# One transformer block on one core: the order of the attention steps chosen by the next piece of side work, and paired maxima in every unit from the third on

## The chip, the cores and the metric

The kernel runs on 1 core of one Trainium2 chip. The metric is the device time of one execution in microseconds (us), given as the median over several executions. A core has five engines that run side by side and meet only at semaphores: TensorE (PE in the profile, its weight loads PEld), VectorE (DVE), ScalarE (ACT), GpSimd (POOL) and SyncE (SP, which here issues DMAs). Matrix products land in PSUM, which has eight banks of 128 partitions by 512 fp32 numbers; DVE and ACT read them from there, POOL and the DMAs can't.

## The reference

A block with adaptive layer norm: attention over 2048 rows of width 576 with 32 heads of 18 columns, then a gated feed-forward layer with 4608 hidden columns.

```
mod = (silu(c) @ w_mod) -> sa, ca, ga, sb, cb, gb
h = layernorm(x) * (1 + ca) + sa
q, k, v = split(h @ wqkv)             # 32 heads of 18
p = softmax(q @ k.T * 18 ** -0.5)     # 2048 x 2048 for each head
x = x + ga * ((p @ v) @ wo)
h = layernorm(x) * (1 + cb) + sb
x = x + gb * ((sigmoid(h @ w_gate) * (h @ w_up)) @ w_down)
```

The softmax needs the maximum of each row of scores before the exponentials can be taken. The kernel works in fp32 accuracy; where it uses the faster fp32r products, an operand is split into a high and a low part.

## The kernel before

**Units and steps.** Attention goes in 32 units. A unit is two heads and one half (1024) of the query rows; units 0 to 15 hold the first half of the rows, 16 to 31 the second. A unit has 16 steps (`kt`), one for each 128 keys. A step makes four score tiles of 128 keys by 512 queries (two heads, two query chunks, L1016) and takes their exponentials on ACT (L1020); the products with the values (L585) follow two steps behind (`LAG`). Units pass in the loop `for u in range(UNITS)`, steps in `for kt in range(NT)`. Each odd step closes a pair of steps, and the order of the work in the even and in the odd step is written out as a string of letters:

- `t`: one score tile and its exponential. `m`: one turn of the maxima (below).
- `v`: the products with the values for a whole step; `a`, `b`: the same for the first and the second 256 queries of each chunk.
- `w`, `s`: a place where side work is put in. `c`: the rest of that side work. `k`: the copy of the finished accumulator `o` out of PSUM on ACT (L602, `taken`), which is due once in a unit.

TensorE and ScalarE run in the order of the program here (`manual_schedule`); the order on VectorE and GpSimd is chosen by the framework's scheduler.

**Three orders.** `PLAIN` units use `("vtmmttmvtm", "tmttkwmctmm")`, `HALVED` units `("vmmtmmtsactt", "wmcmbkttmtmt")`, and units 30 and 31 a third one with `TURNED`. The tuples at the head of the file fix which unit is which: halved are 1 to 15 and 21 to 27.

**Maxima.** The generator `maxima` (L455 on) runs ahead of attention by one unit and 24 turns: a turn is one score tile of 128 queries by 512 keys, computed the other way round (L480), and its maximum on DVE (L486). Four turns belong to a step, so eight to a pair. In a unit outside `SINGLE`, two of the eight chunks are paired: the first is a product with differences of keys, ACT takes its positive part into `over` (L489), and one DVE instruction adds this to the second chunk and takes the maximum (L491). So a paired group of eight costs DVE seven instructions and ACT one more; an unpaired one costs DVE eight. `SINGLE` holds units 0, 1, 17 to 20 and 29. At the end of a unit `spread` (L507 on) transposes the maxima and sends them by DMA into the rows of the query tile.

**Banks.** Score tiles, maxima tiles and all side work take turns in seven PSUM banks (`bank`), in order of issue: a new tile has to wait until the tile seven before it has been read. The eighth bank is the accumulator `o`.

**Side work.** `outputs` (four transposes, L612) brings a finished unit's result into rows at step 3 of the next unit. From step 240 (`FROM0`, unit 15) on, one piece of `first_rows` is taken in each pair of steps: eleven pieces that load and split the output weights on POOL (`load_wo`); for each of the 8 row tiles of the first half four pieces of `project_o` (transposes of the row tile, L699, and their copy by DVE, L705; one more transpose, L716; two groups of 14 products, L732, each ended by a DVE addition, L734); eight pieces of statistics; the scales of the layer norm, whose power runs on POOL (L196); and twelve sets of four transposes (L842) with pieces on POOL between them. From step 457 (`FROM1`, unit 28) on, the pieces of `last_rows_project` follow: three for each of the 8 row tiles of the second half (three transposes, then two groups of 9 products). In a pair all of this stands in the odd step, at `w`.

Of the kernel before, what the change touches and what calls it, by code (L numbers as in the profile page):

```python
# [37 lines left out]
HW = S // 2  # L38
UNITS = H
LEAD = 6  # L40
FROM0, FROM1 = 15 * 16, 28 * 16 + 9
DL = 384
ORDER = (1, 6, 2, 7, 5, 4, 3)
LOOK = 4
# [2 lines left out]
LAG = 2  # L47

MAXIMA = ((1, 0), (0, 0), (1, 1), (0, 2), (1, 2), (0, 3), (0, 1), (1, 3))
PLAIN = (0, 16, 17, 18, 19, 20, 28, 29)  # L50
SINGLE = (0, 1, 17, 18, 19, 20, 29)
HALVED = tuple(range(1, 16)) + tuple(range(21, 28))
MAXIMA_H = ((1, 0), (0, 0), (1, 1), (0, 2), (0, 3), (1, 2), (0, 1), (1, 3))
SIDES_H = ((1, 0), (1, 1), (0, 1), (0, 0))
SIDES = ((0, 0), (0, 1), (1, 0), (1, 1))
TURNED = ((0, 1), (0, 0), (1, 1), (1, 0)), ((0, 1), (1, 1), (0, 0), (1, 0))
ORDERED = 7
SEVENS = NB - 2
TURNS = {1: 1, 6: 2, 2: 4, 7: 3, 5: 5, 4: 7, 3: 6}
# [5 lines left out]
def tile_block(ctx, tc, x_in, wqkv, wo, w_gate, w_up, w_down, c_in, w_mod, out):  # L65
# [389 lines left out]
    def maxima():  # L455


        n = HW // P
        last = None
        for u in range(UNITS):  # L460
            qs, ks = heads(u)
            mx = mxs[u % 2]
            if u not in SINGLE and u - 2 in SINGLE:
                nc.gpsimd.memset(mx[:, 0:n, 1], LOWEST)
            for i in range(8 * n):
                if last is not None and i == (9 if u == 1 else 8):
                    if u == 1:
                        for _ in spread(*last):
                            pass
                    else:  # L470
                        state["spread"] = last
                qt = i // 8
                beside = (64 * u + i - 64 - 4 * LEAD) // 64
                pairs = u not in SINGLE or u in (17, 29) and beside in HALVED
                h, kc = (MAXIMA_H if beside in HALVED else MAXIMA)[i % 8]
                rows = slice(64 * h, 64 * h + 3 * DH)
                paired = pairs and h == 0 and kc < 2
                at = NCH if paired and kc == 0 else kc
                sp = bank()
                nc.tensor.matmul(  # L480
                    sp, qs[rows, qt * P : (qt + 1) * P],
                    ks[rows, at * 512 : (at + 1) * 512], start=True, stop=True,
                )
                to = mx[:, h * n + qt, kc : kc + 1]
                if not paired:
                    nc.vector.tensor_reduce(to, sp, axis=AX.X, op=ALU.max)  # L486
                elif kc == 0:
                    over = small.tile([P, 512], F32, name="over", bufs=1)
                    nc.scalar.activation(over, sp, AF.Relu)  # L489
                else:  # L490
                    nc.vector.tensor_tensor_reduce(  # L491
                        out=over, in0=sp, in1=over, scale=1.0, scalar=LOWEST,
                        op0=ALU.add, op1=ALU.max, accum_out=mx[:, h * n + qt, 0:1],
                    )
                if i < 8 * n - 1:
                    yield
            nm = small.tile([P, 2, n], F32, name="nm")
            nc.vector.tensor_reduce(
                nm.rearrange("p h t -> p (h t)"), mx, axis=AX.X, op=ALU.max, negate=True
            )  # L500
            last = (qs, nm)
            yield
        for _ in range(8):
            yield
        state["spread"] = last
# [175 lines left out]
    def project_o(t):  # L681

        wo_h, wo_l, we = weights
        if t <= 8:
            held_rows[:] = temp([P, 2048], F32R), temp([P, 2048], F32)
        T, T_ = held_rows
        if t < 8:
            xt, full, od = T_[:, 0:D], T_[:, 1024:1536], T_[:, 1536:1664]
        else:
            T, T_ = T[:, 1024 * (t % 2) : 1024 * (t % 2) + 1024], T_[:, 960 * (t % 2) : 960 * (t % 2) + 960]  # L690
            xt, full = T_[:, 0:D], T_[:, D : D + 384]
        nc.gpsimd.dma_start(xt, x_rows[:, t, :])
        src = Os[t // 8][:, t % 8, :]
        n = 4 if t < 8 else DL // P
        oh = T[:, 0 : n * P]
        ol = T[:, 512 : 512 + n * P]
        pt = bank()
        for i in range(n):
            nc.tensor.transpose(pt[:, i * P : (i + 1) * P], src[:, i * P : (i + 1) * P], ident)  # L699
        if t >= 12:  # L700
            nc.vector.tensor_copy(oh, pt[:, 0 : n * P])
            nc.vector.tensor_sub(ol, pt[:, 0 : n * P], oh.bitcast(F32))
        else:
            full = full[:, 0 : n * P]
            nc.vector.tensor_copy(full, pt[:, 0 : n * P])  # L705
            nc.gpsimd.tensor_copy(oh, full)
            nc.gpsimd.tensor_sub(ol, full, oh.bitcast(F32))
        yield
        if t < 8:
            om = T[:, 1024:1152]  # L710
            omh = T[:, 1152:1280]
            nc.gpsimd.tensor_copy(
                od.rearrange("p (a e) -> p a e", e=64), src[:, DM:D].unsqueeze(1).to_broadcast([P, 2, 64])
            )
            pt = bank()
            nc.tensor.transpose(pt[:, 0:P], od, ident)  # L716
            nc.vector.tensor_copy(od, pt[:, 0:P])
            nc.gpsimd.tensor_copy(om[0:64], od[0:64])
            nc.gpsimd.tensor_copy(omh[64:P], od[64:P])
            nc.gpsimd.tensor_sub(om[64:P], od[64:P], omh[64:P].bitcast(F32))  # L720
            yield
        for h in range(2):
            cols = slice(h * HALF, (h + 1) * HALF)
            ts_ = []
            for i in range(n):
                a, b = oh[:, i * P : (i + 1) * P], ol[:, i * P : (i + 1) * P]
                ts_ += [(a, wo_h[:, i, cols]), (a, wo_l[:, i, cols]), (b, wo_h[:, i, cols])]
            if t < 8:
                ts_ += [(om, we[:, 0, cols]), (om, we[:, 1, cols])]
            acc = bank()  # L730
            for i, (a, w) in enumerate(ts_):
                nc.tensor.matmul(acc[:, :HALF], a, w, start=i == 0, stop=i == len(ts_) - 1)  # L732
            to = Oa[:, t, :] if t < 8 else xt
            nc.vector.tensor_add(to[:, cols], xt[:, cols], acc[:, 0:HALF])  # L734
            yield
        if t >= 8:
            nc.gpsimd.dma_start(x1p[:, t - 8, :], xt)

# [227 lines left out]
    for u in range(UNITS):  # L966
# [6 lines left out]
        for kt in range(NT):  # L973
            step = u * NT + kt
            turns["to"] = 64 + 4 * LEAD + 4 * (step + 1)
            kcols = slice(kt * P, (kt + 1) * P)
            plain = u in PLAIN
            halved = u in HALVED
            sides = iter(SIDES if plain else SIDES_H if halved else TURNED[kt % 2])
            probs = [None] * 4  # L980
            order = ("vtmmttmvtm", "tmttkwmctmm") if plain else ("vmmttmmtvt", "mtkttmwmcmt")
            if halved:
                order = ("vmmtmmtsactt", "wmcmbkttmtmt")
            for does in order[kt % 2]:
                if does == "m":
                    turn()
                elif does == "k":
                    taken()
                elif does == "w":
                    if kt == 3:  # L990
                        follow.append(outputs())
                        next(follow[-1], None)
                    if "spread" in state and not halved:
                        follow.append(spread(*state.pop("spread")))
                        next(follow[-1])
                    if FROM0 <= step < FROM1:
                        next(rows0, None)
                    if step >= FROM1:
                        next(rows1, None)
                elif does == "s":  # L1000
                    if "spread" in state:
                        follow.append(spread(*state.pop("spread")))
                        next(follow[-1])
                elif does == "c":
                    while follow:
                        next(follow.pop(0), None)
                elif does == "v":
                    if step >= LAG:
                        values()
                elif does in "ab":  # L1010
                    values(slice(0, 256) if does == "a" else slice(256, 512))
                else:
                    c, h = next(sides)
                    sT = bank()
                    rows = slice(64 * h, 64 * h + 3 * DH + 2)
                    nc.tensor.matmul(  # L1016
                        sT, ks[rows, kcols], qs[rows, c * 512 : (c + 1) * 512], start=True, stop=True
                    )
                    pr = probs[2 * c + h] = ppool.tile([P, 512], F32, name=f"p{2 * c + h}")
                    state["exp"] = nc.scalar.activation(pr, sT, AF.Exp, scale=SCALE)  # L1020
# [678 lines left out]
```

## Time and profile before

| | us |
|---|---|
| median of 3 executions | 2830.45 |
| lowest, highest | 2825.56, 2831.19 |
| the profiled execution | 2833.97 |
| its span, first to last instruction | 2832.2 |

The profiled execution stands 3.5 us above the median. Its span has three parts: normalising and the projections to q, k and v up to about 237 us, attention up to about 1555 us, and the feed-forward layer after that. The page gives for each engine the time in which it was busy and its share of the span; the groups of instructions give busy time, mean duration of one in ns, and the idle time in front of them with what ended it. The chain is the sequence of work that ended last, followed back from the end. A windows row gives, for one stretch of the span, its length, the busy time of each engine with the number of instructions, the granted TensorE clock and the share of the DMA engines. Matrix products overlap in the pipeline, so their single durations are longer than the spacing at which they follow each other.

### The profile page before, as it was taken

The page shows a single profiled execution, that of the slowest core. Times are in us where ns is not written, and L with a number is a line of the kernel's source. Part 1 is how long each engine was busy: PE and PEld are TensorE (multiplying, and loading weights), DVE is VectorE, ACT ScalarE, POOL GpSimd, SP SyncE. Part 2 cuts the span into 40 slices and gives each one's busy share as a digit, 9 for nine tenths or more (in the row PEclk, how much of TensorE's full clock was granted, in tenths as well). Part 3 has the DMA queues.
Part 4 walks back from the last instruction along what each step waited for, and adds up shares of the span by engine and source line. Part 5 has one row for each costly group of instructions (what it writes and reads, how often), then busy time and mean ns, then how long its engine had stood idle before and what let it go on. Part 6 is the DMA issues. An engine that isn't in the chain of part 4 may idle for free.

```text
span 2832.2 us, 50132 instructions
## 1 busy us (share of the span) xinstructions
PE 2788.0 (98%) x18293; PEld 1843.5 (65%) x18293; DVE 2315.3 (82%) x4367; ACT 1592.1 (56%) x3020; POOL 821.5 (29%) x1088
## 2 busy tenths in 40 slices
PE   7999999999999999999999999999999999999999
PEld 5974444444444444444443888888888888888888
DVE  7278999999998988999982878888898677777777
ACT  3216999999997678999888322333333222222221
POOL 3125208787842111662013222222221100000000
PEclk9999999999999999999999999999999999999999
DMA  5344225544432120221125866667767966666663
GB/s 171 126 150 148 69 58 171 171 171 164 181 108 78 36 58 23 105 100 58 36 75 176 295 212 226 236 216 272 275 249 275 351 200 195 199 198 196 199 198 111
DMA packets 170119, 462.55 MB, mean 163 GB/s; under 512 B 21196, under 2 KB 87760, under 8 KB 159760
## 3 DMA queue, kind: packets, MB, share of 16 engines
q1 hardware_dynamic: 148768, 358.36, 37.8%
q0 software_dynamic: 21104, 100.98, 10.0%
q8 instruction: 144, 2.36, 0.3%
q14 instruction: 103, 0.84, 0.1%
HBM read 281.92 MB, written 176.82 MB: 162 GB/s over the span
## 4 chain that ended last, share of the span: by engine, by line
PE 92%; DVE 4%; DMA 2%; ACT 1%; issue 1%; POOL 0%; SPq 0%; DVEq 0%; POOLq 0%; ACTq 0%
PE x L1145 26%; PE o L585 19%; PE s L1016 12%; PE s L480 11%; PE d L1295 8%; PE d L1227 6%; PE s L301 4%; PE s L732 2%; PE s L352 2%; DMA out_dram<-Oa 1%; PE s L612 1%; DVE mx L486 1%; ACT p L1020 1%; DVE Oa L1299 0%; DMA wm<-in_w_mod_dram 0%
## 5 line engine op out<-in xcount | busy, mean ns | idle before, releaser
L1020 ACT ACTIVATE p<-s 128x512 f32<-128x512 f32 x2048 | 1075.0, 620 | 134.5 <-PE s L1016 74.3
L486 DVE TENSOR_REDUCE mx<-s 128x1 f32<-128x512 f32 x1636 | 1033.2, 684 | 103.3 <-PE s L480 88.6
L585 PE MATMUL o<-p,vaug 128*32 128x256 f32 (+1 forms) x5504 | 587.6, 497 | 5.0 <-ACT oT L602 4.6
L480 PE MATMUL s<-k,q 54*128 54x512 f32 x1920 | 533.7, 434 | 1.9 <-DVE mx L486 1.6
L1016 PE MATMUL s<-q,k 56*128 56x512 f32 x1920 | 533.1, 446 | 0.2
L1016 PEld LDWEIGHTS s<-q,k 56*128 56x128 f32 x1920 | 257.9, 185 | 275.8 <-DVE mx L486 99.7
L480 PEld LDWEIGHTS s<-k,q 54*128 54x128 f32 x1920 | 281.6, 185 | 213.2 <-DVE mx L491 146.7
L1145 PE MATMUL x<-k,w 128*128 128x512 f32 x1512 | 369.7, 392 | 2.4 <-ACT w L1126 2.4
L1145 PEld LDWEIGHTS x<-k,w 128*128 128x128 f32 x1512 | 276.9, 188 | 55.1 <-ACT w L1126 2.6
L1295 PE MATMUL d<-wd,hh 128*128 128x288 f32 x1280 | 256.5, 295 | 3.0 <-DVE Oa L1299 2.4
L1145 PE MATMUL x<-big,w 128*128 128x512 f32 x1008 | 247.0, 394 | 1.8 <-DVE u L1604 1.8
L1145 PE MATMUL x<-w,w 128*128 128x512 f32 x1008 | 245.3, 391 | 0.0
L585 PEld LDWEIGHTS o<-p,vaug 128*32 128x32 f32 x5504 | 109.6, 108 | 206.5 <-issue 131.0
L1295 PEld LDWEIGHTS d<-wd,hh 128*128 128x128 f32 x1280 | 207.2, 188 | 7.4 <-DVE Oa L1299 3.1
L1145 PEld LDWEIGHTS x<-big,w 128*128 128x128 f32 x1008 | 186.3, 189 | 38.4 <-DVE u L1604 2.4
L1145 PEld LDWEIGHTS x<-w,w 128*128 128x128 f32 x1008 | 184.3, 188 | 34.5
L1295 PE MATMUL d<-wd,hl 128*128 128x288 f32 x640 | 189.1, 295 | 0.2 <-DVE hl L1174 0.2
L1299 DVE TENSOR_TENSOR Oa<-Oa,d 128x288 f32<-128x288 f32 x320 | 140.1, 453 | 55.8 <-PE d L1295 51.9
L1303 POOL DMA_DIRECT2D out_dram<-Oa x16 | 8.7, 545 | 584.7 <-DVE Oa L1299 584.5
L491 DVE CUSTOM_DVE_ANT_0 over<-s,over 128x512 f32<-128x512 f32 x206 | 141.4, 687 | 0.2
L1154 ACT ACTIVATE sg<-x 128x512 f32<-128x512 f32 x36 | 21.6, 600 | 210.9 <-PE x L1145 210.8
L1126 ACT CAST w<-S 128x768 fp32r<-128x768 f32 x72 | 60.2, 838 | 134.0 <-POOL S L1104 133.2
(262 smaller groups left out, 3996.4 us busy)
## 6 DMA issues: line engine op xcount, KB each, us to landing
ws<-w SPq DMA_DIRECT2D x126, 640.0 KB
w<-ws SPq DMA_DIRECT2D x126, 640.0 KB
wd<-wds SPq DMA_DIRECT2D x19, 1152.0 KB
k<-kd SPq DMA_DIRECT2D x60, 360.0 KB
wds<-w POOLq DMA_DIRECT2D x18, 1152.0 KB, 5.3
wtd<-t POOLq DMA_DIRECT2D x32, 576.0 KB, 4.7
wt<-wtd SPq DMA_DIRECT2D x64, 288.0 KB
wd<-wds SPq DMA_DIRECT2D x52, 288.0 KB
```

Source lines behind the costliest of these rows:

```text
L301: nc.tensor.matmul(acc, w, hT[:, t, cols], start=n == 0, stop=n == len(ts_) - 1)
L480: nc.tensor.matmul(sp, qs[rows, qt * P : (qt + 1) * P], ks[rows, at * 512 : (at + 1) * 512], start=True, stop=True,)
L486: nc.vector.tensor_reduce(to, sp, axis=AX.X, op=ALU.max)
L491: nc.vector.tensor_tensor_reduce(out=over, in0=sp, in1=over, scale=1.0, scalar=LOWEST, op0=ALU.add, op1=ALU.max, accum_out=mx[:, h * n + q ...
L585: nc.tensor.matmul(acc[32 * j : 32 * j + 32, cols], vaug[:, kt, (2 * p + h) * VW : (2 * p + h) * VW + 32], probs[2 * c + h][:, cols], star ...
L1016: nc.tensor.matmul(sT, ks[rows, kcols], qs[rows, c * 512 : (c + 1) * 512], start=True, stop=True)
L1020: state["exp"] = nc.scalar.activation(pr, sT, AF.Exp, scale=SCALE)
L1126: nc.scalar.copy(w[:, :, 0:3, :], src)
L1145: nc.tensor.matmul(acc[v], w[:, v, a, :], X[s][:, b, :], start=first and n == 0, stop=n == 6, skip_group_check=not first,)
L1227: nc.tensor.matmul(acc, a[:, rows], w[:, k, :], start=n == 0, stop=n == 2)
L1295: nc.tensor.matmul(acc[:, :HALF], a[:, f, rows], w[:, f, cols], start=n == 0, stop=n == 5)
L1299: nc.vector.tensor_add(Oa[:, t, cols], Oa[:, t, cols], acc[:, :HALF])
```

## The change

The order is no longer fixed for a unit. Before each even step the program sets `state["halved"]`: it holds in every unit but unit 0, except where the last piece of side work yielded `"g"`. `project_o` yields `"g"` in front of each of its two groups of products. So a pair of steps that will take a group of products has the plain order, and all other pairs, with other pieces or none, have the halved order. The third order and `TURNED` are gone.

- In a halved pair the piece of side work moves from `w` (the head of the odd step) to `s` (in the even step, in front of `a`). `outputs` stays at `w`.
- In the plain odd step the accumulator's copy `k` and the place `w` come earlier: `tmttkwmctmm` becomes `ktmwttmctmm`.
- `SINGLE` is now `(0, 1)`: the maxima of units 17 to 20 and 29 are paired too, also beside plain steps. The order of the eight chunks follows the order of the pair beside which they run.
- `FROM1` is one step earlier (456, even), since a halved pair takes its piece in the even step.

The pieces themselves, their number and their order are as before. The diff:

```diff
--- before.py
+++ after.py
@@ -38,7 +38,7 @@
 HW = S // 2
 UNITS = H
 LEAD = 6
-FROM0, FROM1 = 15 * 16, 28 * 16 + 9
+FROM0, FROM1 = 15 * 16, 28 * 16 + 8
 DL = 384
 ORDER = (1, 6, 2, 7, 5, 4, 3)
 LOOK = 4
@@ -47,13 +47,10 @@
 LAG = 2
 
 MAXIMA = ((1, 0), (0, 0), (1, 1), (0, 2), (1, 2), (0, 3), (0, 1), (1, 3))
-PLAIN = (0, 16, 17, 18, 19, 20, 28, 29)
-SINGLE = (0, 1, 17, 18, 19, 20, 29)
-HALVED = tuple(range(1, 16)) + tuple(range(21, 28))
+SINGLE = (0, 1)
 MAXIMA_H = ((1, 0), (0, 0), (1, 1), (0, 2), (0, 3), (1, 2), (0, 1), (1, 3))
 SIDES_H = ((1, 0), (1, 1), (0, 1), (0, 0))
 SIDES = ((0, 0), (0, 1), (1, 0), (1, 1))
-TURNED = ((0, 1), (0, 0), (1, 1), (1, 0)), ((0, 1), (1, 1), (0, 0), (1, 0))
 ORDERED = 7
 SEVENS = NB - 2
 TURNS = {1: 1, 6: 2, 2: 4, 7: 3, 5: 5, 4: 7, 3: 6}
@@ -470,9 +467,8 @@
                     else:
                         state["spread"] = last
                 qt = i // 8
-                beside = (64 * u + i - 64 - 4 * LEAD) // 64
-                pairs = u not in SINGLE or u in (17, 29) and beside in HALVED
-                h, kc = (MAXIMA_H if beside in HALVED else MAXIMA)[i % 8]
+                pairs = u not in SINGLE
+                h, kc = (MAXIMA_H if state.get("halved") else MAXIMA)[i % 8]
                 rows = slice(64 * h, 64 * h + 3 * DH)
                 paired = pairs and h == 0 and kc < 2
                 at = NCH if paired and kc == 0 else kc
@@ -705,7 +701,7 @@
             nc.vector.tensor_copy(full, pt[:, 0 : n * P])
             nc.gpsimd.tensor_copy(oh, full)
             nc.gpsimd.tensor_sub(ol, full, oh.bitcast(F32))
-        yield
+        yield None if t < 8 else "g"
         if t < 8:
             om = T[:, 1024:1152]
             omh = T[:, 1152:1280]
@@ -718,7 +714,7 @@
             nc.gpsimd.tensor_copy(om[0:64], od[0:64])
             nc.gpsimd.tensor_copy(omh[64:P], od[64:P])
             nc.gpsimd.tensor_sub(om[64:P], od[64:P], omh[64:P].bitcast(F32))
-            yield
+            yield "g"
         for h in range(2):
             cols = slice(h * HALF, (h + 1) * HALF)
             ts_ = []
@@ -732,7 +728,7 @@
                 nc.tensor.matmul(acc[:, :HALF], a, w, start=i == 0, stop=i == len(ts_) - 1)
             to = Oa[:, t, :] if t < 8 else xt
             nc.vector.tensor_add(to[:, cols], xt[:, cols], acc[:, 0:HALF])
-            yield
+            yield None if h else "g"
         if t >= 8:
             nc.gpsimd.dma_start(x1p[:, t - 8, :], xt)
 
@@ -974,33 +970,26 @@
             step = u * NT + kt
             turns["to"] = 64 + 4 * LEAD + 4 * (step + 1)
             kcols = slice(kt * P, (kt + 1) * P)
-            plain = u in PLAIN
-            halved = u in HALVED
-            sides = iter(SIDES if plain else SIDES_H if halved else TURNED[kt % 2])
+            if kt % 2 == 0:
+                state["halved"] = u > 0 and state.get("next") != "g"
+            halved = state["halved"]
+            sides = iter(SIDES_H if halved else SIDES)
             probs = [None] * 4
-            order = ("vtmmttmvtm", "tmttkwmctmm") if plain else ("vmmttmmtvt", "mtkttmwmcmt")
-            if halved:
-                order = ("vmmtmmtsactt", "wmcmbkttmtmt")
+            order = ("vmmtmmtsactt", "wmcmbkttmtmt") if halved else ("vtmmttmvtm", "ktmwttmctmm")
             for does in order[kt % 2]:
                 if does == "m":
                     turn()
                 elif does == "k":
                     taken()
-                elif does == "w":
+                elif does in "ws":
                     if kt == 3:
                         follow.append(outputs())
                         next(follow[-1], None)
-                    if "spread" in state and not halved:
+                    if "spread" in state and halved == (does == "s"):
                         follow.append(spread(*state.pop("spread")))
                         next(follow[-1])
-                    if FROM0 <= step < FROM1:
-                        next(rows0, None)
-                    if step >= FROM1:
-                        next(rows1, None)
-                elif does == "s":
-                    if "spread" in state:
-                        follow.append(spread(*state.pop("spread")))
-                        next(follow[-1])
+                    if step >= FROM0 and halved == (does == "s"):
+                        state["next"] = next(rows0 if step < FROM1 else rows1, None)
                 elif does == "c":
                     while follow:
                         next(follow.pop(0), None)
```

## The prediction

> **What bounds the kernel now.** I read the page first: busy shares and chain, then the two attention groups.
>
> ```profile
> PE 2788.0 (98%) x18293; PEld 1843.5 (65%) x18293; DVE 2315.3 (82%) x4367; ACT 1592.1 (56%) x3020; POOL 821.5 (29%) x1088
> PE 92%; DVE 4%; DMA 2%; ACT 1%; issue 1%; POOL 0%; SPq 0%; DVEq 0%; POOLq 0%; ACTq 0%
> L1020 ACT ACTIVATE p<-s 128x512 f32<-128x512 f32 x2048 | 1075.0, 620 | 134.5 <-PE s L1016 74.3
> L486 DVE TENSOR_REDUCE mx<-s 128x1 f32<-128x512 f32 x1636 | 1033.2, 684 | 103.3 <-PE s L480 88.6
> ```
>
> TensorE carries 92% of the chain, but a busy PE also counts products that are waited for in the pipeline. Spacing says more than the mean: an exponential takes ACT 1075.0 / 2048 = 0.525 us, a maximum takes DVE 1033.2 / 1636 = 0.632 us. Then I cut attention into units, at the first exponential of each: units 15 to 20, 23, 26 and 28 (length, then busy time of PE, PEld, DVE, ACT, POOL).
>
> ```profile
> 818.90:856.80 37.90, 37.90 (x325) 15.58 (x317) 34.83 (x68) 36.67 (x75) 18.07 (x21) 1.00 0.26 73
> 856.80:902.60 45.80, 44.67 (x300) 20.05 (x298) 42.49 (x74) 34.40 (x68) 12.33 (x20) 1.00 0.27 84
> 902.60:953.60 51.00, 50.23 (x331) 24.00 (x329) 44.51 (x82) 34.70 (x68) 8.46 (x17) 0.97 0.15 45
> 953.60:1003.00 49.40, 48.61 (x329) 23.61 (x327) 44.41 (x82) 34.50 (x67) 8.46 (x18) 1.00 0.14 43
> 1003.00:1052.50 49.50, 48.81 (x329) 23.83 (x328) 43.12 (x83) 35.72 (x71) 8.46 (x18) 1.00 0.16 43
> 1052.50:1101.90 49.40, 46.95 (x298) 20.57 (x299) 39.90 (x84) 38.05 (x77) 10.48 (x15) 0.97 0.11 34
> 1181.50:1223.20 41.70, 41.70 (x345) 17.90 (x341) 38.46 (x72) 37.42 (x76) 28.17 (x34) 1.00 0.22 77
> 1303.20:1341.60 38.40, 38.40 (x329) 15.75 (x325) 35.38 (x68) 37.18 (x76) 0.82 (x2) 1.00 0.14 41
> 1379.60:1423.70 44.10, 43.04 (x287) 18.74 (x285) 39.96 (x71) 35.57 (x71) 4.97 (x9) 1.00 0.17 51
> ```
>
> A halved unit without row work (unit 26) takes 38.4 us, ACT busy for 37.2 of them. The five plain units 16 to 20 take 245.1 us, 53.1 more than five halved ones: that is where the change acts. Last the chain, where rows of L585 are the value products, so that one pair of steps reaches from its first such row to the next pair's (units 15 and 16):
>
> ```profile
> 841.04 1.00 PE o L585 x8
> ...
> 845.72 1.00 PE o L585 x8
> ...
> 855.29 0.99 PE o L585 x8
> 857.20 1.00 PE o L585 x8
> ...
> 866.55 0.99 PE o L585 x8
> ...
> 871.60 1.00 PE o L585 x8
> ...
> 876.83 1.00 PE o L585 x8
> ...
> 880.65 0.26 PE s L716
> ...
> 882.20 0.99 PE o L585 x8
> ...
> 884.10 1.00 PE o L585 x8
> ...
> 886.00 2.06 PE s L732 x14
> ...
> 888.72 1.00 PE o L585 x8
> ```
>
> A halved pair takes 845.72 - 841.04 = 4.68, a plain one without row work 871.60 - 866.55 = 5.05: eight maxima of 0.632 make 5.06, so DVE bounds it. A plain pair with fourteen products takes 888.72 - 882.20 = 6.52, and TensorE has no gap in it: there DVE and ACT have time to spare.
>
> **The change, part by part.**
>
> *Pairs without products become halved and paired (units 16 to 20).* Eleven pieces of weights precede (no TensorE work), then eight row tiles of four pairs: transposes (halved), one transpose (halved), products, products (plain), then statistics. So 24 of 40 pairs turn halved. I start from five halved units, 5 x 38.4 = 192.0, and add what TensorE gets on top, because a halved pair keeps it full too: its ACT work is nine instructions of 0.525 = 4.73, no less than the pair. The four transposes cost what they cost in a halved pair of unit 23, here in the chain:
>
> ```profile
> 1206.20 1.00 PE o L585 x8
> ...
> 1208.08 0.57 PE o L585 x8
> 1208.65 0.43 PE s L1016 x2
> 1209.08 0.59 PE s L842 x4
> ...
> 1211.60 1.07 PE o L585 x8
> ```
>
> The set is 0.59, so 8 x 0.59 = 4.7; the single transpose is 0.26, 8 x 0.26 = 2.1. The product pairs stay at 6.52, 16 x (6.52 - 4.68) = 29.4. One stall remains in unit 20: the power on POOL holds DVE, TensorE stands, and its clock is halved afterwards.
>
> ```profile
> 1074.78 1.69 POOL r L196
> ```
> ```profile
> 1077.31 0.51 PE L480 MATMUL s<-k,q 54*128 54x512 f32 x2 [1.63 <-DVE mx L486]
> ```
> ```profile
> 1078.10:1081.60 3.50, 3.50 (x18) 1.03 (x14) 2.91 (x7) 1.41 (x3) 0.00 (x0) 0.51 0.00 0
> ```
>
> I keep 1.69 for it and half of 3.5, 1.7, for the clock: 3.4. Sum 192.0 + 4.7 + 2.1 + 29.4 + 3.4 = 231.6 against 245.1: 13.5 less. Unit 15's window is 0.5 under a halved unit's only because a plain pair's first exponential comes sooner; that comes back: 13.0.
>
> *Pairing in the plain pairs that stay.* It takes one maximum (0.632) from DVE and gives ACT one instruction of about 0.525. Neither is the bound, so nothing; but ACT can now be late in front of the products. Unit 29 is plain and paired already:
>
> ```profile
> 1440.19 1.00 PE o L585 x8
> 1442.09 0.99 PE o L585 x8
> ...
> 1444.27 1.39 PE s L732 x9
> ...
> 1446.33 1.00 PE o L585 x8
> ```
>
> From the second value products to the row's products it takes 1444.27 - 1442.09 = 2.18; unpaired it took 886.00 - 884.10 = 1.90. So pairing costs up to 0.28 in the old order. The new odd step asks ACT for one exponential before `w` instead of three, and the other two follow while the 2.06 us of products are past; I take 6.52, nearest the gapless row. Both ends: 0 and 16 x 0.28 = 4.5 slower. For the eight product pairs of units 28 and 29, which pay the 0.28 now, I take half back, 1.1.
>
> *Pieces at `s` instead of `w`.* In unit 23 a set of transposes makes a pair 1211.60 - 1206.20 = 5.40, and the unit is 41.7 - 38.4 = 3.3 longer for four sets: 0.82 each, of which 0.59 is TensorE. At `w` the set splits four score products into two and two; at `s` it stands directly ahead of `a` and splits nothing. I take 0.59, 12 x 0.23 = 2.8 less; ends: nothing, and as much slower. All that a piece issues moves with it by half a pair: its copies on DVE, the casts on POOL, and POOL's load of the input row, which waits for the tile before, whose products now also stand earlier. From a set at `s` to its products at `w` lie the rest of one pair and most of the next, over 5 us, against one pair of 5.05 or more before, so POOL's cover grows. The four DMAs of `spread` on SP stay in their pair, the seventh of eight, so that all of the eighth still lies between them and the unit that needs them.
>
> *Units 28 to 31.* The first four pairs of unit 28 turn halved: 4 x (5.05 - 4.68) = 1.5. The wait for the accumulator's copy at a plain unit's start goes there:
>
> ```profile
> PE o L585 <- ACT oT L602: 2.7, 4, 0.8
> ```
>
> that is 2.7 / 4 = 0.7 (the starts of units 17 to 20; in a halved pair the copy is ahead of time, as unit 26's sum shows). The 0.5 at the switch comes off: 1.7. The other pairs exchange plain for halved at equal cost; units 30 and 31 leave the third order, which I set at nothing, within 1 us to either side.
>
> *The copy first.* Only the starts of units 29 and 31 are still plain, so it is worth at most 2 x 0.7; I count nothing. If it were late, it would hold the exponentials queued behind it on ACT and the next unit's first products. Removing three small memsets on POOL costs nothing: POOL is idle for most of these units.
>
> **Sum.** 13.0 + 2.8 + 1.1 + 1.7 = 18.6. Against the profiled execution's own 2833.97 this gives 2815.4; that execution stands 3.5 above the median, so the median goes from 2830.45 to 2812. Everything before unit 15 and after attention keeps its order and its time. Own range of this case: all kinds of small ends (the 3.4 gone; sets at 0.82) give 2805 to 2817. The Trainium skill (TensorEngine Tiling (Array Packing), Key Properties) says that a change of tiling mode drains TensorE, which speaks against the halved order with its two half-size value groups. The trace agrees: the halves take 0.57 + 0.57 where one group takes 1.00, a loss of 0.14 a pair, which the 4.68 holds already.
>
> **The rivals.** *Smaller gain.* ACT stays late before the products (4.5), the 1.1 isn't had, and sets cost 0.82 at `s` as well (2.8 in units 21 to 25, 8 x 0.23 = 1.8 in 16 to 20): 18.6 - 10.2 = 8.4 less, 2822. For it speaks unit 29; against it, that `w` moved ahead of two exponentials.
>
> *No change.* Each of 16 row tiles brings one switch from halved to plain and back. A halved pair ends on an exponential, and the next plain pair's second value products need it: if ACT runs behind, TensorE waits. At 18.6 / 16 = 1.2 us each the gain is gone: 2830. Against it speaks the one such switch in the trace: at 855.29 the second group follows after 1.91, as in steady plain pairs (884.10 - 882.20 = 1.90).
>
> *Slower.* The same wait, of 1.2, and each time the clock drops as it did at 1078: 1.7 more, 16 x 2.9 = 46 - 18.6, so 2858. From 1.5 us for a switch on the kernel is slower by more than 0.2%. For it: an idle of 1.63 was followed by half clock. Against it: the same switch without a wait. By the Trainium skill (TensorE: Matmul & The Clock Gate, Part 1: The HAM clock gate) the clock falls after an idle window of about 3.4 us; by that rule such short waits would cost no clock, and this rival would end at the one before. The trace doesn't bear that out: 1.63 us were enough once.
>
> **How the numbers follow.** About 0.2%, 5.7 us, is what a measurement of this kernel can tell from no change. Chances: the forecast 0.55, smaller gain 0.23, no change 0.10, slower 0.12. The first two are faster by over 0.2% (below 2824.8) nearly whole: faster 0.77, same 0.11, slower 0.12. The range reaches from the forecast's low end past the smaller gain: 2805 to 2827.
>
> **What would show it.** Units 16 to 20 at about 232 us in sum; L491 and L489 240 times, L486 1568 times; halved pairs with a set at about 5.3 and product pairs at 6.5; the sets of L842 no longer between two pairs of score products; no half clock in unit 17. It is wrong if TensorE waits for `p` at the second value products after a switch, if ACT's `over` stands ahead of the row's products, or if the scheduler puts copies for the side work into VectorE's queue ahead of maxima that free banks.

## The result: slower, by stalls that the forecast did not list

The changed kernel takes 2836.43 us (median; 2833.41 to 2846.33) against 2828.81 for the kernel before, measured beside it. The ratio is 1.003, with a 95% interval of 1.0023 to 1.0037. The forecast was 2812. The profiled execution took 2834.49 us, with a span of 2832.7. That is only 0.5 us above the profiled execution of before, but attention ended 5.1 us later in it (its last exponential at 1557.7 for 1552.6); what lies behind attention took 1275.0 us for 1279.5, though nothing was changed there.

The page of the changed kernel first: busy shares, and the rows of the maxima and of their products, which now wait; the last row is these products in the kernel before.

```profile
PE 2776.2 (98%) x18613; PEld 1835.7 (65%) x18613; DVE 2300.3 (81%) x4367; ACT 1608.0 (57%) x3054; POOL 822.1 (29%) x1085
L482 DVE TENSOR_REDUCE mx<-s 128x1 f32<-128x512 f32 x1568 | 995.4, 684 | 131.0 <-PE s L476 115.9
L476 PE MATMUL s<-k,q 54*128 54x512 f32 x1920 | 511.3, 429 | 16.0 <-DVE mrows L512 7.8
L480 PE MATMUL s<-k,q 54*128 54x512 f32 x1920 | 533.7, 434 | 1.9 <-DVE mx L486 1.6
```

(The changed file is shorter, so lines moved: L482 was L486, L476 was L480, L1009 was L1020, L581 was L585, L728 was L732, L507 to L512 are `spread`, L608 to L624 `outputs`.) The 34 further pairs of maxima are there, 1636 - 1568 = 2 x 34. New is the idle time in front of L476: 16.0 us where L480 had 1.9. The windows of units 16 to 20, 23, 28, 29 and 30, cut as before at each unit's first exponential:

```profile
855.80:900.80 45.00, 43.80 (x347) 19.62 (x339) 38.95 (x76) 37.65 (x77) 11.29 (x18) 1.00 0.21 62
900.80:952.70 51.90, 49.47 (x360) 23.66 (x359) 41.12 (x82) 38.06 (x76) 8.42 (x16) 0.97 0.14 43
952.70:1003.10 50.40, 47.97 (x360) 23.29 (x359) 41.07 (x82) 38.02 (x76) 8.41 (x16) 1.00 0.16 44
1003.10:1055.00 51.90, 49.47 (x360) 23.68 (x359) 41.17 (x82) 38.25 (x77) 8.41 (x16) 0.97 0.15 43
1055.00:1101.90 46.90, 44.38 (x342) 19.87 (x345) 38.28 (x83) 37.70 (x76) 9.79 (x14) 0.96 0.11 35
1181.10:1222.20 41.10, 41.10 (x345) 17.14 (x343) 38.32 (x72) 37.62 (x76) 29.15 (x35) 1.00 0.23 78
1378.30:1421.30 43.00, 41.53 (x333) 17.82 (x325) 37.05 (x72) 37.01 (x75) 4.98 (x8) 1.00 0.15 50
1421.30:1474.50 53.20, 50.49 (x343) 23.31 (x340) 40.16 (x76) 38.88 (x78) 7.18 (x12) 0.94 0.18 58
1474.50:1520.30 45.80, 43.19 (x312) 18.92 (x310) 27.69 (x54) 36.42 (x73) 12.87 (x20) 1.00 0.44 115
```

Units 16 to 20 take 246.1 us, 1.0 more than before and 14.5 more than forecast; unit 29 grew from 48.4 to 53.2. DVE's load fell (44.4 to 41.1 in unit 18) and the time did not follow. Cut into pairs of steps, each from its first exponential to the next pair's, the loss sits in few places. In unit 18 the pairs take 4.51, 8.51, 6.97, 5.43, 4.43, 6.47, 8.83 and 5.23 us; the second holds `outputs` and a group of products, the seventh `spread` and a group of products. The sixth, a group of products alone, is the 6.5 of the forecast. (The prediction cut pairs at the value products; by that cut the sixth takes 6.51, and the stalls are the same.) What TensorE's products wait for in units 16 to 20 of the changed kernel:

```profile
PE s L476 <- DVE mrows L512: 4.8, 4, 1.2
PE s L476 <- ACT oT L624: 4.7, 4, 1.2
PE s L1005 <- DVE mx L482: 1.3, 1, 1.3
```

The last is the power on POOL, known from before. The first two are new: four times TensorE waits for the tile that `spread` transposed into, four times for that of `outputs`. Here is one of them, on ACT, in order of time:

```profile
990.01 2.08 ACT L1009 ACTIVATE p<-s 128x512 f32<-128x512 f32 x4
993.81 1.08 ACT L1009 ACTIVATE p<-s 128x512 f32<-128x512 f32 x2 [1.73 <-PE s L1005]
994.78 0.24 ACT L511 CAST mrows<-s 16x128 fp32r<-16x128 f32 x1
```

and on TensorE:

```profile
991.00 0.28 PE L507 MATMUL s<-ident,nm 128*16 128x128 f32 x1
991.16 1.86 PE L728 MATMUL s<-w,t 128*128 128x288 f32 x12
992.86 0.43 PE L728 MATMUL s<-we,t 128*128 128x288 f32 x2
993.21 0.50 PE L1005 MATMUL s<-q,k 56*128 56x512 f32 x2
```
```profile
995.39 0.50 PE L476 MATMUL s<-k,q 54*128 54x512 f32 x1 [1.21 <-DVE mrows L512]
```

The transpose L507 is done at 991.28. Its copy L511 is `c`, and in the new string two exponentials stand ahead of `c` in ACT's queue. The scores of these exponentials come behind the fourteen products on TensorE. So ACT idles for 1.73 us with the copy in its queue, starts it at 994.78, and DVE's part ends at 995.33. Until then one of the seven banks is held, and the tile that comes round to it, L476, lets TensorE stand for 1.21. The Trainium skill (PSUM — Partial Sum Buffer, Engine vs sequencer instructions) calls ScalarE's queue strictly first in, first out; the trace agrees, with 1.73 us of idle ahead of an instruction whose data had been ready.

### The profile page after: what moved, and what is told of

Read it like the earlier page. It is cut to its first block, busy times and chain, and to the rows that moved or that the text cites. A ratio compares the mean times of both kernels' runs of the same rounds, so it can differ in the third digit from the quotient of the medians.

```text
span 2832.7 us, 50849 instructions
## 1 busy us (share of the span) xinstructions
PE 2776.2 (98%) x18613; PEld 1835.7 (65%) x18613; DVE 2300.3 (81%) x4367; ACT 1608.0 (57%) x3054; POOL 822.1 (29%) x1085
## 4 chain that ended last, share of the span: by engine, by line
PE 92%; DVE 4%; DMA 1%; ACT 1%; issue 1%; SPq 0%; POOL 0%; DVEq 0%; POOLq 0%; ACTq 0%
PE x L1134 26%; PE o L581 19%; PE s L1005 12%; PE s L476 11%; PE d L1284 8%; PE d L1216 6%; PE s L298 4%; PE s L728 2%; PE s L349 2%; ACT p L1009 1%; PE s L608 1%; DVE mx L482 1%; DVE w L1124 0%; DMA wm<-in_w_mod_dram 0%; DVE Oa L1288 0%
## 5 line engine op out<-in xcount | busy, mean ns | idle before, releaser
L1009 ACT ACTIVATE p<-s 128x512 f32<-128x512 f32 x2048 | 1080.5, 624 | 115.4 <-PE s L1005 91.2
L482 DVE TENSOR_REDUCE mx<-s 128x1 f32<-128x512 f32 x1568 | 995.4, 684 | 131.0 <-PE s L476 115.9
L581 PE MATMUL o<-p,vaug 128*32 128x256 f32 (+1 forms) x5824 | 595.6, 481 | 3.0 <-ACT p L1009 3.0
L476 PE MATMUL s<-k,q 54*128 54x512 f32 x1920 | 511.3, 429 | 16.0 <-DVE mrows L512 7.8
L1005 PE MATMUL s<-q,k 56*128 56x512 f32 x1920 | 519.0, 451 | 1.3 <-DVE mx L482 1.3
L476 PEld LDWEIGHTS s<-k,q 54*128 54x128 f32 x1920 | 279.9, 186 | 250.0 <-DVE mx L487 163.5
L1005 PEld LDWEIGHTS s<-q,k 56*128 56x128 f32 x1920 | 248.6, 185 | 246.4 <-issue 109.6
L581 PEld LDWEIGHTS o<-p,vaug 128*32 128x32 f32 x5824 | 115.1, 108 | 210.0 <-issue 132.4
L487 DVE CUSTOM_DVE_ANT_0 over<-s,over 128x512 f32<-128x512 f32 x240 | 164.7, 686 | 1.2 <-PE s L1005 0.3
L485 ACT ACTIVATE over<-s 128x512 f32<-128x512 f32 x240 | 150.8, 628 | 15.3 <-PE s L476 15.3
```

Of the source, the lines that this page charges most:

```text
L476: nc.tensor.matmul(sp, qs[rows, qt * P : (qt + 1) * P], ks[rows, at * 512 : (at + 1) * 512], start=True, stop=True,)
L487: nc.vector.tensor_tensor_reduce(out=over, in0=sp, in1=over, scale=1.0, scalar=LOWEST, op0=ALU.add, op1=ALU.max, accum_out=mx[:, h * n + q ...
L581: nc.tensor.matmul(acc[32 * j : 32 * j + 32, cols], vaug[:, kt, (2 * p + h) * VW : (2 * p + h) * VW + 32], probs[2 * c + h][:, cols], star ...
L1005: nc.tensor.matmul(sT, ks[rows, kcols], qs[rows, c * 512 : (c + 1) * 512], start=True, stop=True)
```

## Experiments

Theory 1 is this: the bank is held because `c` now stands behind exponentials that wait for the products. The rivals were that pairing loads ACT (theory 2), and that the earlier place of `w` starves it (theory 3). All ratios are to the kernel before, with 95% intervals.

**One letter moved.** The order of TensorE's products is unchanged.

```diff
-("vtmmttmvtm", "ktmwttmctmm")
+("vtmmttmvtm", "ktmwcttmtmm")
```

> The changed kernel with one letter moved: in the plain odd step the rest of the side work (c) stands directly behind w, not behind two score tiles and a turn. The order of the products on TensorE stays exactly the same; only ACT's and DVE's emptying of the transposes' bank is issued earlier. Theory 1 (a bank of the ring of seven is held: the transposes of outputs and of spread are emptied by ACT behind two exponentials whose scores wait behind the fourteen products): the pairs that now take 8.5 to 9.5 us (second pair of units 17 to 20) and 8.8 us (seventh pair of units 16 to 19) fall to 6.5 to 7, no wait of TensorE for oT L624 or mrows L512 is left, and the kernel is some 20 us faster than the changed one, 0.993 to 0.995 of the kernel before. Theory 2 (the positive part that pairing gives to ACT makes it late in the plain pairs): no more than 3 us gained, since pairing stays. Theory 3 (the place w itself, ahead of two exponentials, starves ACT): no more than 3 us gained, since w stays.

Measured: 2810.06 against 2830.63 us, 0.9925 (0.9913 to 0.9937). In unit 18 the second pair fell from 8.51 to 6.84, the seventh from 8.83 to 7.11. Units 16 to 20 in this run:

```profile
856.20:899.70 43.50, 43.46 (x347) 19.65 (x342) 38.66 (x76) 37.68 (x76) 11.93 (x18) 1.00 0.22 66
899.70:946.90 47.20, 47.12 (x360) 23.20 (x360) 40.63 (x82) 38.08 (x76) 8.41 (x16) 1.00 0.16 47
946.90:994.20 47.30, 47.21 (x360) 23.19 (x360) 40.70 (x82) 38.16 (x77) 8.41 (x16) 1.00 0.15 47
994.20:1041.40 47.20, 47.12 (x360) 23.22 (x359) 40.57 (x82) 38.14 (x76) 8.41 (x16) 1.00 0.16 46
1041.40:1085.80 44.40, 43.08 (x342) 19.80 (x346) 38.13 (x83) 37.92 (x76) 9.77 (x14) 1.00 0.12 36
```

Now PE's busy time fills the windows but for the power's stall in unit 20. The copy stands at 984.51, while the products run, and ACT's idle comes behind it (ACT in order of time):

```profile
982.60 2.07 ACT L1009 ACTIVATE p<-s 128x512 f32<-128x512 f32 x4
984.51 0.24 ACT L511 CAST mrows<-s 16x128 fp32r<-16x128 f32 x1
986.37 1.58 ACT L1009 ACTIVATE p<-s 128x512 f32<-128x512 f32 x3 [1.63 <-PE s L1005]
```

ACT idles nearly as long as in the changed kernel, 1.63 for 1.73; only the order changed. That rules out theories 2 and 3 as the main cause: pairing and `w` stayed. This version beats both kernels.

**The odd step of before, all else changed.**

```diff
-("vtmmttmvtm", "ktmwttmctmm")
+("vtmmttmvtm", "tmttkwmctmm")
```

> The changed kernel with the plain odd step of before (tmttkwmctmm): k and w late, c one turn behind w. Theory 1: the held banks are gone as well, the second and seventh pairs come back to about 6.5 to 7 us; ACT is asked for three exponentials before w, and where maxima are paired a product pair can cost up to 0.28 us more (16 pairs, 4.5 us), so 0.993 to 0.997 of the kernel before. Theory 2: still slower than before (1.002 or more), since pairing stays. Theory 3: like theory 1, but better than the run with only c moved.

Measured: 0.9947 (0.9935 to 0.9958). The stalls are gone here too. But a product pair alone takes 6.83 where it takes 6.5 with `w` early. So the early `w` was a gain; what spoiled it was that `c` did not come along.

**The new odd step alone, in the kernel before.**

```diff
-            order = ("vtmmttmvtm", "tmttkwmctmm") if plain else ("vmmttmmtvt", "mtkttmwmcmt")
+            order = ("vtmmttmvtm", "ktmwttmctmm") if plain else ("vmmttmmtvt", "mtkttmwmcmt")
```

> The kernel before with only the plain odd step changed to ktmwttmctmm; units, pairing and the halved order as before. Theory 1: the held banks come with the letters alone: units 16 to 20, 28 and 29 have six or seven starts with outputs and as many spreads in plain pairs, each about 2 us, 20 to 30 us slower, ratio 1.007 to 1.011. Theory 2: nothing to within 3 us, as no pairing is added. Theory 3: slower too, but then in every product pair and not only in the second and the seventh of a unit.

Measured: 1.0051 (1.0037 to 1.0065), less than expected. What TensorE waits for in units 16 to 20:

```profile
PE s L480 <- ACT oT L628: 5.0, 4, 1.2
PE s L480 <- DVE mrows L516: 4.8, 4, 1.2
```

These are the same stalls, and no pair of these units is halved. Units 16 to 18 run no paired maxima either (of these five units, unit 19 is the first in which L491 runs), and they hold five of the eight stalls: the string alone makes them. The second pair of unit 18 went from 6.85 to 8.64, the seventh from 6.84 to 8.29. What the copy `k` gains stands against them: the first pair fell from 6.14 to 5.55, which I had left out of this expectation.

**The changed kernel, unpaired.**

```diff
-SINGLE = (0, 1)
+SINGLE = (0, 1, 17, 18, 19, 20, 29)
```

> The changed kernel with the maxima of units 17 to 20 and 29 unpaired again; orders as changed. Theory 1: the stalls at the second and seventh pair stay (TensorE waits for oT L624 and mrows L512), the halved pairs without products are bound by eight maxima on DVE (5.05 us for 4.68), so slower than the changed kernel by 3 to 10 us: 1.004 to 1.007 of the kernel before. Theory 2: the stalls go, 0.995 to 0.998.

Measured: 1.0068 (1.0056 to 1.008). The stalls stay, 4.8 and 4.7 us in units 16 to 20 as in the changed kernel, in units 16 to 18 with no paired maxima beside them, and the rest gets slower. Theory 2 is out.

**`c` behind one exponential.**

```diff
-("vtmmttmvtm", "ktmwttmctmm")
+("vtmmttmvtm", "ktmwtctmtmm")
```

> The changed kernel with c one place earlier in the plain odd step (ktmwtctmtmm): the emptying of the transposes' bank stands behind one exponential, not two. If the held bank's time sets the stall, it shrinks by about one exponential and the pitch of the copy, 0.5 to 0.7 us a time: TensorE's wait of 1.2 us for mrows and oT falls to about 0.6, the second pairs of units 17 to 20 from 8.5 to about 7.8, the seventh from 8.8 to about 8.2, fewer half-clock stretches, 0.996 to 1.000 of the kernel before, between the changed kernel (1.003) and the one with c directly behind w (0.9925). If the place in the queue counts only as a whole (late or not), it is like one of these two.

Measured: 0.9988 (0.9979 to 0.9997). The ratio is in the expected place, but not for the expected reason: in unit 18 the second pair fell to 8.02 and the seventh only to 8.66, while the waits became shorter.

```profile
PE s L476 <- DVE mrows L512: 4.2, 4, 1.0
PE s L476 <- ACT oT L624: 2.8, 4, 0.7
```

So the cost comes mostly in one step, not in equal ones: a single exponential ahead of `c` is enough to make the copy wait for the products. The second adds 0.5 us in the second pair and 0.2 in the seventh. A part of the gain is the clock's: unit 18, with no half clock in either execution, gained 0.7 us (50.4 to 49.7), and unit 17, which had it in the changed kernel, 2.2 (51.9 to 49.7). In the profiled execution no half clock followed any of the twelve stalls; but it was the longest of ten (2831.45 us, median 2826.36), so the clock's share in the median is not shown.

**Pairing alone, in the kernel before.**

```diff
-SINGLE = (0, 1, 17, 18, 19, 20, 29)
+SINGLE = (0, 1)
```

> The kernel before with the maxima of units 17 to 20 and 29 paired, orders and places as before. By the forecast's parts: pairs of steps without products lose DVE's eighth maximum (5.05 to about 4.7, some 28 pairs, 8 to 10 us less), product pairs gain up to 0.28 us (16 pairs, up to 4.5 more): 4 to 8 us less, 0.997 to 0.9985. If ACT is no bound in the old order, 8 to 10 less, 0.9965. If ACT is late everywhere in plain pairs, no gain, 1.000.

Measured: 1.001 (1.0001 to 1.0019), no gain. In plain pairs, pairing is worth nothing in sum: three pairs with transposes in unit 18 became shorter by 0.15 to 0.27 us, three of the four product pairs longer by 0.25 to 0.34. ACT's extra instruction comes ahead of products that now wait for it, as unit 29 had shown. And the plain pair without row work in unit 16, which the prediction took to be bound by eight maxima on DVE, keeps its length with seven, 872.31 - 867.25 = 5.06 us for 5.05:

```profile
867.25 0.99 PE o L585 x8
872.31 0.97 PE o L585 x5
```

In the kernel before, TensorE's weights had stood in that pair for an exponential:

```profile
870.61 0.18 PEld L1016 LDWEIGHTS s<-q,k 56*128 56x128 f32 x1 [0.44 <-ACT p L1020]
```

So DVE was at most one of two bounds in that pair, and taking one of its maxima away gained nothing there. One more stretch of half clock, in unit 28, adds to it in the profiled execution.

**`w` a score tile later, `c` behind it.**

```diff
-("vtmmttmvtm", "ktmwttmctmm")
+("vtmmttmvtm", "ktmtmwcttmm")
```

> The changed kernel with the plain odd step ktmtmwcttmm: c directly behind w, and w one score tile and one turn later, so that two exponentials are asked for before the products (one in the changed order, three in the old). If each exponential before w makes a paired product pair longer (6.5 us with one, 6.83 with three), pairs of about 6.65 and 0.9930 to 0.9940. If only the run of score tiles behind the products counts, the shorter run here (four for six) frees the ring and it is as good as with c alone moved or better, 0.9915 to 0.9925.

Measured: 0.9954 (0.9942 to 0.9967), slower than both expectations. The chain shows where it goes, ahead of the products:

```profile
932.26 0.42 PE s L1005
932.69 0.24 PE s L476 x2
932.92 0.23 PE s L1005 x2
933.15 0.41 PE s L476
933.57 2.06 PE s L728 x14
```

The six score tiles before `w` take 933.57 - 932.26 = 1.31 us, the last of them 0.41. The weights of this last tile waited for an exponential, which stood behind `over` on ACT:

```profile
933.06 0.18 PEld L476 LDWEIGHTS s<-k,q 54*128 54x128 f32 x1 [0.31 <-ACT p L1009]
```

With `w` two tiles earlier four tiles stand before it, and a pair with products alone takes 6.47 for 6.83. The loss is not proportional to the exponentials before `w`: two cost as much as three (6.83 in the run with the old odd step), and both orders put six tiles before `w`.

**All pairs halved.**

```diff
-state["halved"] = u > 0 and state.get("next") != "g"
+state["halved"] = u > 0
```

> The changed kernel with every pair of steps from unit 1 on in the halved order, products too (at s, ahead of a). By TensorE's sum a product pair would take 4.68 + 2.06 + a switch, about 6.8, with c directly behind the half group a, no bank held: then 16 + 16 pairs a little longer than with c alone moved (6.5, 5.85), 0.994 to 0.996. If ACT, with eight exponentials and the paired tile behind each other, can't make up the 2 us without scores, product pairs take 7.3 or more, 1.000 or above.

Measured: 0.9951 (0.9938 to 0.9965). Product pairs take 6.68, and no stall of a held bank appears, since `c` stands directly behind `a`, or one turn behind `w`. So the choice of order by the coming piece is worth 0.9951 to 0.9925 once its plain order is sound, and was a loss as it was made.

**The accumulator's copy late.** In the kernel with `c` behind `w`:

```diff
-("vtmmttmvtm", "ktmwcttmtmm")
+("vtmmttmvtm", "tmwcttkmtmm")
```

> The kernel with c directly behind w, and in it the accumulator's copy k back behind the second exponential after w (tmwcttkmtmm); the products keep their order. The copy falls due in a plain pair only at the starts of units 29 and 31; if its place matters as it did in the plain units before (0.7 us of waiting for a start), at most 1.4 us slower than with the copy first, 0.9925 to 0.9935 of the kernel before. If the copy first was needed for more than that (it delays the next unit's products and the ring), units 29 and 31 grow by 2 us or more each and the ratio is above 0.994.

Measured: 0.9944 (0.9932 to 0.9957). TensorE in units 29 to 31 of this run waits for the copy:

```profile
PE o L581 <- ACT oT L598: 2.7, 2, 1.5
```

The two plain starts grew from 5.83 to 7.09 and from 5.13 to 6.68, 2.8 us in sum, twice the bound that I had set. It is more than that in the median, 0.9944 for 0.9925. In the profiled execution the rest lies in unit 20, 46.8 us for 44.4, with half clock for 6.8 us behind the power, which the run with the copy first did not have; whether it lies there in the other executions stays open.

**The kernel with `c` behind `w`, unpaired.**

```diff
-SINGLE = (0, 1)
+SINGLE = (0, 1, 17, 18, 19, 20, 29)
```

> The kernel with c directly behind w, and the maxima of units 17 to 20 and 29 unpaired again. If pairing is worth something in the halved pairs only, there DVE's eight maxima bound a pair (5.05 for 4.68): 20 to 24 pairs beside which those units' maxima run, 7 to 9 us slower than the paired one, and product pairs stay at 6.5: 0.995 to 0.996 of the kernel before. If pairing also speeds the product pairs, those grow too and the ratio is above 0.997; if it is worth nothing, 0.9925.

Measured: 0.9976 (0.9967 to 0.9986). Pairing is worth 0.9976 to 0.9925 here, more than expected. Product pairs alone stay at 6.48, so the reason that I had attached to a ratio above 0.997 is wrong: the loss is in the others. A pair with four transposes went from 5.43 to 6.01, one without row work from 4.67 to 5.08, and units 15 and 27 pay 1.1 and 1.2 us as well. The kernel before had paired the maxima that run there, the first 24 turns of units 17 and 29 (its L491 ran 206 times: 25 units of eight, and six more), so this run takes away 2.3 us more than the change had brought.

## Why the prediction was wrong

*The step that failed* is the first part of the change, where I started from five halved units and added "16 x (6.52 - 4.68)" for the product pairs. The halved base carries `outputs` and `spread` at the price of the halved order. In the plain order they meet the products, and there the string also moves `c`: from one turn behind `w` to two score tiles and a turn behind it. I listed `k`, `w`, POOL's queue and SP's, but not the letter between. The missing term is a stall of 1.7 us (unit 18's seventh pair, 8.83 for 7.11), twelve times: eight in units 16 to 20 and four in 28 to 30, for which TensorE's waits are

```profile
PE s L476 <- DVE mrows L512: 2.9, 2, 1.5
PE s L476 <- ACT oT L624: 2.4, 2, 1.2
```

That is 20.4 us, an estimate, since the pair behind a stall can win a little back (5.23 for 5.43 in unit 18). Besides, five stretches of half clock, each 3.4 us long, fell into attention, up to 1.7 us each. Measured, the last exponential of attention ended 1557.7 us into the span for 1531.1 with the one letter moved: 26.6. The forecast's gain of 18.6 less 26.6 is a loss of 8.0, beside the measured 7.6.

*What held.* With the stall taken away, units 16 to 20 take 229.6 us where the forecast had 231.6, and the kernel 2810 where it had 2812. A product pair alone is 6.5, as taken from the unpaired row, and not the 6.8 that the 0.28 of unit 29 would have made: `w` ahead of two exponentials does remove it. The power's stall was set at 3.4; the pair that holds it took 7.96 for 4.69 in the changed kernel, so 3.3. With the one letter moved no half clock followed it, and the pair took 6.78, 2.1 over 4.69: 1.3 of the 2.0 us by which 229.6 lies below the forecast are luck with the clock. Sets of transposes at `s` made pairs of 5.22 where they had made 5.47; the gain in units 21 to 25 was 1.8 us, with 2.8 forecast.

*What was mis-sized.* Unit 28 was to gain 1.7 and half of 0.28 twice; without the stall it gained 3.0 (44.1 to 41.1). Units 30 and 31, set at nothing to within 1 us, lost 1.0. The copy first, counted as nothing with a bound of 1.4, is worth 2.8 at the two plain starts. Pairing was right at "nothing" in the plain pairs, but its main worth, some 12 us in the pairs around them (the 14 us of the last run less 2.3), I had not stated as its own term. That DVE alone bounds a plain pair was a misreading; the price of 5.05, taken from rows, did not suffer by it.

*The rivals.* "Slower" came true, but by another mechanism than the one I gave. At the second value products after a switch from halved to plain TensorE did not wait in units 16 to 29. In units 30 and 31 it did, twice, 0.31 and 0.26 us, far from 1.2 each time:

```profile
1515.20 1.07 PE L581 MATMUL o<-p,vaug 128*32 128x512 f32 x8 [0.31 <-ACT p L1009]
```

The second half of that rival was right: the clock fell after short idles. The list of what would make the prediction wrong had three cases and none was this one; the nearest said that copies for the side work might come late in VectorE's queue. They came late in ScalarE's, and by the written order, not by the scheduler.

## What to carry to other kernels

When work is moved ahead in a written order, look up for each buffer it fills the instruction that empties it, and ask what now stands ahead of that instruction in its own queue, and whether this waits for the very work that was moved. Most of the cost here was the wait for the moved work (one exponential ahead of `c` brought 1.55 of the seventh pair's 1.72 us), not the time of the instructions that were jumped. A price taken from rows of one order holds for the letters that were in it; a pair in which two kinds of side work meet needs a row of its own.

## Hardware: half clock after short idles

The granted clock was half of full speed in these stretches of the changed kernel's attention (3.5 us at a mean of 0.51, so 3.4 us at half each):

```profile
912.40:915.90 3.50, 3.50 (x18) 1.03 (x14) 1.54 (x3) 1.04 (x3) 0.31 (x1) 0.51 0.00 0
1014.80:1018.30 3.50, 3.50 (x18) 1.03 (x14) 1.63 (x3) 1.23 (x3) 0.22 (x1) 0.51 0.00 0
1083.00:1086.50 3.50, 3.50 (x22) 1.12 (x14) 3.39 (x13) 2.22 (x5) 0.00 (x0) 0.51 0.00 0
1434.60:1438.10 3.50, 3.50 (x20) 1.61 (x21) 2.35 (x4) 1.58 (x3) 0.77 (x2) 0.51 0.33 88
1465.30:1468.80 3.50, 3.50 (x18) 1.02 (x14) 1.69 (x3) 1.29 (x3) 0.00 (x0) 0.51 0.02 4
```

Four of them follow four of the twelve stalls, in which TensorE was idle for 1.2 to 1.5 us; the third follows the power's, 1.3 us. Eight stalls of the same length were followed by none. With `c` one place earlier, idles of up to 1.0 in units 16 to 20, no stall of the twelve was followed by one, and the run with only `c` moved directly behind `w` had none in attention. But a shorter idle is no safeguard. In the kernel before, 0.64 us of waiting for the accumulator's copy at the start of unit 17 came just ahead of half clock:

```profile
907.16 1.70 PE L585 MATMUL o<-p,vaug 128*32 128x512 f32 x8 [0.64 <-ACT oT L602]
907.40:910.90 3.50, 3.50 (x18) 1.03 (x14) 1.93 (x5) 1.43 (x4) 0.02 (x1) 0.51 0.47 144
```

The same 0.64 at the starts of units 18 and 19 did not. (The forecast's sign "no half clock in unit 17" failed: the changed kernel has it there again, at 912.4.) The Trainium skill (TensorE: Matmul & The Clock Gate, Part 1: The HAM clock gate) names an idle window of about 3.4 us for the fall; these idles were far shorter, so here the measurement decides. What decides which of these idles is followed by half clock, these runs don't settle.
